# Two stores per block, behind the first or behind the second transposing transfer of a retention and MLP kernel

## The chip, the cores and the metric

The kernel runs on one core of a Trainium2 chip. The metric is the device time of one launch in microseconds (us). Before the change the median of three runs is 190.57 us (190.29 to 191.04).

## The reference

Per batch and head a state of 64 x 64 is decayed and fed with an outer product of k and v, position by position; q reads it. The heads are then put side by side, and an MLP with the activation h * tanh(softplus(h)) follows.

```python
batch, n_heads, seq, head_dim = (4, 8, 768, 64)
...
for t in range(S):
    state = gamma * state + einsum('bhd,bhe->bhde', k[:, :, t], v[:, :, t])
    y[:, :, t] = scale * einsum('bhd,bhde->bhe', q[:, :, t], state)
...
x = y.transpose(0, 2, 1, 3).reshape(B * S, H * D)     # 3072 x 512
h = x @ w_in                                          # 512 -> 2048
sp = where(h > 20.0, h, log1p(exp(minimum(h, 20.0))))
out = (h * tanh(sp)) @ w_out                          # 2048 -> 512
```

Inputs and output are fp32; the products inside are made from fp16 operands.

## The kernel before, in words

**Chunks and blocks.** The 768 positions of a batch are 6 chunks of 128 positions with all 8 heads, so there are 24 chunks (`NCK`), numbered g. A block is the unit of the MLP: block 0 has four chunks, blocks 1 to 10 have two each, and `first[b]` is a block's first chunk (`first[4]` = 10, `first[5]` = 12, and so on). `ONE` = 3, `BACK` = 4 and `DEFER` = 6 are numbers of blocks at which the order changes.

**A chunk's way in.** SP (SyncE) issues a chunk's loads of q, k and v from HBM (`load_one`, L174; tiles `qf`, `kf`, `vf`, four buffers each). GpSimd casts them to fp16 with their scales (`casts_qk`: q on L440, k on L454; `casts_v`: L459). Then SP issues one transposing DMA from the cast q and k to the tile `qkt` (`turn_by_dma`, L464), which gives q and k with head dimensions on the partitions. It waits for the cast of k. The scores (`score`, L507, tile `at`) and the products with the state (`past_of`, `y_mm` L621) read `qkt`; the outer products (`u_ps`, L515) read the cast k and v.

**A block from number 4 on.** The main loop calls `second_of(blk - 1)`, then `full_in`, then `full_out`. `full_in` makes the hidden layer (`h_ps`, L972, seven products in place of eight by sums of quarters, 112 matmuls) with its activation on ScalarE. `full_out` makes the output (`o_ps`, L1214, seven products of eight matmuls each), and in the midst of it the retention work of coming blocks: `retain(blk + 1, blk + 2)` makes y of the next block and the outer products and scores of the block after that. Sums that need two products run on VectorE, the evacuations on ScalarE and VectorE. TensorE's order is the order in which the program is written.

**The output.** `full_out` takes two tiles `osb` of 128 x 512 fp32 (256 KB, nine buffers), fills them, and appends them to the list `stores`. Nothing is sent to HBM at that place: `store(n)` takes the n oldest of the list and has SP issue them (L1498), and `store_due` takes all that are due (L244). From block 4 on, the two that are taken are those of two blocks before.

**SP's queue.** SP issues in program order, loads, transposing transfers and stores alike; an issue that waits holds what is behind it. Two functions set the order here, with g = `first[blk]` + 6:

- `next_one(g)`, called in the midst of `full_out(blk)`: the transfer of chunk g; in block 6 also the loads of v of two chunks; then two stores (blocks 4 to 7), or all that are due (from block 8 on).
- `second_of(blk)`, called between `full_out(blk)` and `full_in(blk + 1)`: a load, GpSimd's casts of q and k of chunk g + 1, its transfer, GpSimd's casts of v, then two stores in block 3 alone, or all that are due (from block 8 on), and another load.

So blocks 4, 5, 6 and 7 carry the transfers of chunks 16 and 17, 18 and 19, 20 and 21, 22 and 23. The loads of a whole chunk are five DMAs as a rule, and eight for chunks 19 and 21, whose k comes in four parts and whose q comes in two. In block 5, the two loads of `second_of` bring q and k of chunks 20 and 21 alone.

Of the kernel before, what the change touches and what calls it, by code (L numbers as in the profile page):

```python
# [16 lines left out]
def kernel(  # L17
# [15 lines left out]
    NCK = B * NCH  # L33
# [4 lines left out]
    first = [sum(BLOCKS[:i]) for i in range(len(BLOCKS))]  # L38
# [84 lines left out]
    ONE, BACK = 3, 4  # L123
# [40 lines left out]
    def load_one(g, n, queue):  # L164
        b, c = divmod(g, NCH)
        small = g in (first[8] + 1, first[9] + 1)
        if n == 0:
            src, parts = pair_src(q, *divmod(g, 2)), 2 if small else 1
        else:
            src = (k, v)[n - 1][b, :, c * C:(c + 1) * C].rearrange("h p d -> p h d")  # L170
            parts = 1 if g < first[6] else 4 if small and n == 1 else 2
        size = src.shape[1] // parts
        for h in range(0, src.shape[1], size):
            queue.dma_start(loaded[g][n][:, h:h + size], src[:, h:h + size])  # L174

    def load(g):
        room(g)
        for n in range(3):
            load_one(g, n, nc.sync)

    def load_to(g):
        while nload[0] < min(g, NCK):
            load(nload[0])
            nload[0] += 1
# [56 lines left out]
    def store_due(now):  # L241
        while stores and stores[0][0] <= now:
            _, dst, osb = stores.pop(0)
            nc.sync.dma_start(dst, osb)  # L244
# [189 lines left out]
    def casts_qk(g, now=True):  # L434
        qf = loaded[g][0]
        qk16 = castp.tile([P, 2, H, D], FP16, name="qk16", bufs=4)
        q16, k16 = qk16[:, 0], qk16[:, 1]
        v16 = castp.tile([P, H, D], FP16, name="v16", bufs=7)
        heads = slice(g % 2 * (H // 2), (g % 2 + 1) * (H // 2))
        nc.gpsimd.tensor_tensor(  # L440
            in_place(q16.rearrange("p (w x) d -> p w x d", x=2)), by_head(qf),
            scale_by_head(qs_two[:, heads]), op=ALU.mult)
        cast[g] = (q16, k16, v16, qk16)
        if now:
            cast_k(g)
# [12 lines left out]
    def casts_v(g):  # L458
        nc.gpsimd.tensor_tensor(  # L459
            cast[g][2], loaded.pop(g)[2], vs[g % 2].unsqueeze(2).broadcast_to((P, H, D)), op=ALU.mult)  # L460

    def turn_by_dma(g):
        qkt = qktp.tile([P, H, C], FP16, name="qkt", bufs=6)
        nc.sync.dma_start_transpose(qkt, cast[g][3].rearrange("p a h d -> p (a h d)"))  # L464
        qkts[g] = (qkt[:, :HP].rearrange("p (i r) c -> p i r c", r=2), qkt[:, HP:])
# [727 lines left out]
    def full_out(blk, last):  # L1193
# [56 lines left out]
        if last:  # L1250
            mm(px, s(2), t(2))
            u2 = snap(px)
            pb = bank()
            mm(pb, a(0, 1), b(1, 0), True)
            sums_c(blk)
            done(0, 0, pb, m1)
        else:
            leave(new)
            if later is None:
                mm(px, s(2), t(2))  # L1260
                u2 = snap(px)
                retain(new)
            pb = bank()
            mm(pb, a(0, 1), b(1, 0), True, halved=halved[2])
            if later is None:
                sums_c(blk)
                done(0, 0, pb, m1)
                finish(new, False)
            else:
                done(0, 0, pb, m1)  # L1270
                sums_c(blk)
                cast_behind(blk, 3)
                mm(px, s(2), t(2))
                u2 = snap(px)
                retain(new, later)
                mask_two(later)
            next_one(first[blk] + 6)
# [217 lines left out]
    def store(n):  # L1495
        for _ in range(n):
            _, dst, osb = stores.pop(0)
            nc.sync.dma_start(dst, osb)  # L1498
# [8 lines left out]
    def next_one(g):  # L1507
        if g < first[ONE] + 8:
            load_to(g + 3)
        if g < NCK:  # L1510
            turn_by_dma(g)
        if g == first[DEFER] + 6:
            for n in range(2):
                load_one(g + n, 2, nc.sync)
            nload[0] = g + 2
        if g >= NCK:
            store_due(NFB)
        elif g >= first[ONE] + 8:
            store(2)

    def load_qk(g):
        room(g)
# [3 lines left out]
    def second_of(blk):  # L1526
        g = first[blk] + 6
        load, ahead = (load_qk, -1) if blk + 1 == DEFER else (load_to, 0)
        if blk != DEFER:
            load(g + 3 + ahead)  # L1530
        if g < NCK:
            nc.gpsimd.tensor_copy(summed, xts[blk + 1][:, 3, TB - 1:])
            casts_qk(g + 1)
            turn_by_dma(g + 1)
            casts_v(g)
            casts_v(g + 1)
        if blk == ONE:
            store(2)
        elif g >= NCK:
            store_due(NFB)  # L1540
        load(g + 4 + ahead)

# [64 lines left out]
    for blk in range(1, len(BLOCKS)):  # L1607
        last = blk + 1 == len(BLOCKS)
        if blk >= BACK:
            second_of(blk - 1)  # L1610
            full_in(blk, last)
            full_out(blk, last)
            continue
# [5 lines left out]
        for u in range(0 if blk in FULL else NFB // 2):  # L1619
# [7 lines left out]
            for _ in range(SUMS_AT[blk].count(u)):  # L1627
                input_sums.pop(0)()
        later = blk + 2 if blk == ONE else None
        hooks = [([(leave, blk + 1)] if later is not None else []) + [(retain, blk + 1, later)],  # L1630
                 [(next_one, first[blk] + 6)] if blk + 1 >= BACK else
                 [(turn_load, first[blk] + 4)] if blk == 1 else
                 [(turn_four, first[blk] + 4)],
# [35 lines left out]
```

## Time and profile before

| | before |
|---|---|
| median of three runs | 190.57 us (190.29 to 191.04) |
| the profiled execution | 190.19 us, of which the span of instructions 188.4 us |
| TensorE clock granted | 1.00 |
| matmuls / weight loads busy | 182.7 us / 162.9 us |
| VectorE / ScalarE / GpSimd busy | 148.2 / 113.0 / 66.8 us |
| SP's DMA queue | 38.22 MB, 84.9% of the 16 DMA engines' span |

A row of the profile names the line of the kernel, the engine, the operation and the tiles (written <- read). PE is TensorE's matmuls, PEld its weight loads, SPq the queue of SyncE, whose time is the time to issue and not to move the data. All times in the profile count from the first instruction. "DMA to landing" is from the start of the issue to the last byte's signal.

### The profile page before, as it was taken

The page shows a single profiled execution, that of the slowest core. Times are in us where ns is not written, and L with a number is a line of the kernel's source. Part 1 is how long each engine was busy: PE and PEld are TensorE (multiplying, and loading weights), DVE is VectorE, ACT ScalarE, POOL GpSimd, SP SyncE. Part 2 cuts the span into 40 slices and gives each one's busy share as a digit, 9 for nine tenths or more (in the row PEclk, how much of TensorE's full clock was granted, in tenths as well). Part 3 has the DMA queues.
Part 4 walks back from the last instruction along what each step waited for, and adds up shares of the span by engine and source line. Part 5 has one row for each costly group of instructions (what it writes and reads, how often), then busy time and mean ns, then how long its engine had stood idle before and what let it go on. Part 6 is the DMA issues. An engine that isn't in the chain of part 4 may idle for free.

```text
span 188.4 us, 7968 instructions
## 1 busy us (share of the span) xinstructions
PE 182.7 (97%) x3438; PEld 162.9 (86%) x3438; DVE 148.2 (79%) x318; ACT 113.0 (60%) x217; POOL 66.8 (35%) x95
## 2 busy tenths in 40 slices
PE   7998999999999999999999999999999999999993
PEld 7756478888998998998998998998998998988983
DVE  0888599998987998997897697687698698666862
ACT  3575776264555583884684583683673773874651
POOL 5072000588607516532354714714624800000000
PEclk9999999999999999999999999999999999999999
DMA  5999999999899999999799997993999990301103
GB/s 169 306 313 387 387 385 368 298 322 212 171 249 213 188 250 141 175 244 206 197 159 270 192 195 150 181 262 67 218 221 228 203 336 34 117 3 48 67 3 111
DMA packets 83236, 38.84 MB, mean 206 GB/s; under 512 B 58241, under 2 KB 76289, under 8 KB 83201
## 3 DMA queue, kind: packets, MB, share of 16 engines
q1 hardware_dynamic: 82912, 38.22, 84.9%
q8 instruction: 27, 0.44, 1.0%
q10 hardware_dynamic: 288, 0.11, 0.2%
q14 instruction: 9, 0.07, 0.1%
HBM read 27.31 MB, written 6.29 MB: 178 GB/s over the span
## 4 chain that ended last, share of the span: by engine, by line
PE 92%; DMA 3%; SPq 1%; POOL 1%; issue 1%; ACT 0%; DVE 0%; POOLq 0%; DVEq 0%
PE h_ps L972 30%; PE o_ps L1214 23%; PE o_ps L1097 10%; PE h_ps L753 8%; PE o_ps L810 7%; PE y_ps L621 3%; DMA kf<-in_k_dram 3%; PE h_ps L700 2%; PE u_ps L515 1%; PE at L507 1%; PE y_ps L399 1%; POOL qk L320 1%; PE h_ps L736 1%; PE t_ps L267 1%; PE at L350 1%
## 5 line engine op out<-in xcount | busy, mean ns | idle before, releaser
L972 PE MATMUL h_ps<-xt,wsum 128*128 128x128 f16 x576 | 37.5, 219 | 0.0
L984 ACT ACTIVATE g<-h_ps 128x512 f16<-128x512 f32 x54 | 30.8, 599 | 7.1 <-PE h_ps L972 7.1
L972 PEld LDWEIGHTS <-wsum 128*128 128x128 f16 x576 | 33.6, 98 | 0.0
L972 PE MATMUL h_ps<-xt,win 128*128 128x128 f16 x432 | 31.2, 219 | 0.0
L972 PEld LDWEIGHTS <-win 128*128 128x128 f16 x432 | 26.4, 98 | 0.4
L1214 PEld LDWEIGHTS <-gsum 128*128 128x128 f16 x232 | 21.5, 98 | 2.6
L1214 PE MATMUL o_ps<-tmat,gsum 128*128 128x256 f16 (+1 forms) x176 | 21.5, 268 | 0.0
L1045 DVE TENSOR_TENSOR h_ps<-h_ps,hsum 128x512 f32<-128x512 f32 x18 | 12.5, 692 | 9.4 <-PE h_ps L972 9.3
L459 POOL TENSOR_TENSOR v<-vf,qvs 128x512 f16<-128x512 f32 x18 | 19.2, 1082 | 1.1 <-DMA vf<-in_v_dram 1.0
L440 POOL TENSOR_TENSOR qk<-qf,qvs 128x512 f16<-128x512 f32 x18 | 18.9, 1053 | 0.7 <-DMA qf<-in_q_dram 0.7
L1015 ACT COPY h_ps<-h_ps 128x512 f32<-128x512 f32 x18 | 10.5, 582 | 13.4 <-issue 8.6
L1214 PEld LDWEIGHTS <-g 128*128 128x128 f16 x184 | 16.5, 97 | 1.6
L679 ACT CAST xt<-y_ps 128x512 f16<-128x512 f32 x16 | 10.8, 738 | 9.4 <-PE y_ps L621 9.4
L753 PE MATMUL h_ps<-xt,win 128*128 128x256 f16 (+2 forms) x164 | 16.3, 260 | 0.0
L753 PEld LDWEIGHTS <-win 128*128 128x128 f16 x164 | 13.4, 98 | 2.7
L1568 POOL COPY summed<-gsum 128x1 f16<-128x1 f16 x7 | 1.6, 235 | 39.4 <-DVE gsum L933 32.2
L1224 ACT COPY snap<-o_ps 128x256 f32<-128x256 f32 (+1 forms) x22 | 8.2, 374 | 11.0 <-PE o_ps L1214 11.0
L762 ACT ACTIVATE g<-h_ps 128x512 f16<-128x512 f32 x18 | 10.7, 597 | 6.5 <-PE h_ps L753 6.5
L1214 PE MATMUL o_ps<-wout,g 128*128 128x256 f16 (+1 forms) x120 | 14.5, 265 | 0.0
L997 DVE TENSOR_TENSOR hsum<-h_ps,hsum 128x512 f32<-128x512 f32 x18 | 12.3, 685 | 0.9 <-PE h_ps L972 0.2
L454 POOL TENSOR_TENSOR qk<-kf,qvs 128x512 f16<-128x512 f32 x12 | 12.8, 1070 | 0.3 <-DMA kf<-in_k_dram 0.3
L810 PEld LDWEIGHTS <-g 128*128 128x128 f16 x120 | 11.4, 98 | 1.6
(130 smaller groups left out, 348.6 us busy)
## 6 DMA issues: line engine op xcount, KB each, us to landing
out_dram<-osb SPq DMA_DIRECT2D x22, 256.0 KB, 3.7
qf<-in_q_dram SPq DMA_DIRECT2D x18, 256.0 KB, 5.4
kf<-in_k_dram SPq DMA_DIRECT2D x14, 256.0 KB, 5.8
vf<-in_v_dram SPq DMA_DIRECT2D x14, 256.0 KB, 5.3
wt<-in_moe_w_out_dram SPq DMA_DIRECT2D x6, 512.0 KB, 8.6
vf<-in_v_dram SPq DMA_DIRECT2D x20, 128.0 KB, 4.1
wi<-in_moe_w_in_dram SPq DMA_DIRECT2D x4, 512.0 KB, 8.8
kf<-in_k_dram SPq DMA_DIRECT2D x16, 128.0 KB, 4.3
```

What stands on the lines that cost most here:

```text
L440: nc.gpsimd.tensor_tensor(in_place(q16.rearrange("p (w x) d -> p w x d", x=2)), by_head(qf), scale_by_head(qs_two[:, heads]), op=ALU.mult)
L454: nc.gpsimd.tensor_tensor(dst, src, boosts.rearrange("p (w y) -> p w y", y=2).unsqueeze(3).broadcast_to((P, H // 2, 2, D)), op=ALU.mult)
L459: nc.gpsimd.tensor_tensor(cast[g][2], loaded.pop(g)[2], vs[g % 2].unsqueeze(2).broadcast_to((P, H, D)), op=ALU.mult)
L679: nc.scalar.copy(dst[:, :, x], src)
L753: nc.tensor.matmul(h_ps[:, j, cols], wins[s][f // 2][:, bp, f % 2 * P:(f % 2 + 1) * P], xts[blk][:, bp, cols], start=(bp == 0 and at == 0) ...
L810: nc.tensor.matmul(banks[ij][:, t], x(f)[:, t * P:(t + 1) * P], w(f), start=ij in open_banks, stop=f == fs[-1], skip_group_check=True)
L972: nc.tensor.matmul(o_ps[:, f], w(f // 2, k)[:, f % 2 * P:(f % 2 + 1) * P], x[:, k], start=begin and f == 0 and k == 0, stop=k == 1, skip_g ...
L984: nc.scalar.activation(gt[:, f:f + n, j * C:(j + 1) * C], src, AF.Mish, scale=inv_boost3)
L997: nc.vector.tensor_tensor(m, src, plus, op=ALU.add)
L1045: nc.vector.tensor_tensor(pf[p], pa[p], m5[p], op=ALU.add)
L1097: nc.tensor.matmul(o_ps[:, cols], x(f), w(f)[:, cols], start=first and z == 0, stop=z == n - 1, skip_group_check=True)
L1214: nc.tensor.matmul(o_ps[:, c:c + wide], x(f), w(f)[:, c:c + wide], start=first and f == 0 and c == cols.start, stop=f == n - 1, skip_group ...
```

## The change

In blocks 4 to 7 the call `store(2)` leaves `next_one`, where it stood behind the transfer of chunk g, and stands in `second_of`, behind the transfer of chunk g + 1. In block 3 it stood there already. Blocks 8 and later keep `store_due` in both functions. The number of instructions, of DMAs and of bytes stays as it is.

```diff
     def next_one(g):
...
         if g >= NCK:
             store_due(NFB)
-        elif g >= first[ONE] + 8:
-            store(2)
...
     def second_of(blk):
...
             turn_by_dma(g + 1)
             casts_v(g)
             casts_v(g + 1)
-        if blk == ONE:
+        if g < NCK:
             store(2)
-        elif g >= NCK:
+        else:
             store_due(NFB)
         load(g + 4 + ahead)
```

## The prediction

> **What bounds the kernel now.** I began with the page: its engine shares, the chain of work that ended last, and the groups.
>
> ```profile
> span 188.4 us, 7968 instructions
> ...
> PE 182.7 (97%) x3438; PEld 162.9 (86%) x3438; DVE 148.2 (79%) x318; ACT 113.0 (60%) x217; POOL 66.8 (35%) x95
> ...
> PE 92%; DMA 3%; SPq 1%; POOL 1%; issue 1%; ACT 0%; DVE 0%; POOLq 0%; DVEq 0%
> ...
> L1214 PEld LDWEIGHTS <-gsum 128*128 128x128 f16 x232 | 21.5, 98 | 2.6
> ...
> out_dram<-osb SPq DMA_DIRECT2D x22, 256.0 KB, 3.7
> ```
>
> TensorE is busy for 97% of the span and holds 92% of the chain. SP's queue, the one that the change reorders, holds 1% of the chain, and a DMA 3%. So a reordered queue can change the end only where it makes TensorE wait, or ends a wait that TensorE has now. The last two rows are used below: one weight load of the output matmuls takes 98 ns, and one store is 256 KB, so the moved pair is 512 KB.
>
> Next I read the busy time by stretches, for the output halves (`full_out`) of blocks 4 and 7. Each row gives the stretch, its length, then each engine's busy time, the granted clock, the DMA share and GB/s.
>
> ```profile
> 97.00:104.60 7.60, 7.60 (x180) 6.69 (x179) 6.42 (x17) 3.69 (x8) 2.19 (x3) 1.00 0.92 226
> ...
> 138.60:146.00 7.40, 7.40 (x180) 6.53 (x179) 6.48 (x17) 3.63 (x8) 2.19 (x3) 1.00 1.06 228
> ```
>
> TensorE is busy for the whole of both stretches, at clock 1.00. The weight loads fill less, 6.69 of 7.60 us and 6.53 of 7.40 us; what that is worth is weighed under the change. The DMA engines are full too (shares of 0.92 and 1.06 at 226 to 228 GB/s), so a store of 512 KB is not free in DMA time: 0.524 MB at 226 GB/s is 2.3 us of it.
>
> Then the chain in order of time, to see when TensorE reads what the transposing transfers write. Those readers are the `at` matmuls (L507): in block b they score the chunks of block b + 2.
>
> ```profile
> 110.94 3.51 PE o_ps L1214 x32
> 114.45 0.51 PE y_ps L621 x48
> 114.95 0.26 PE u_ps L515 x21
> ...
> 115.25 0.27 PE at L507 x26
> ...
> 115.68 2.73 PE o_ps L1214 x24
> 118.41 6.30 PE h_ps L972 x112
> ...
> 129.08 0.32 PE at L507 x32
> ...
> 142.80 0.29 PE at L507 x32
> ...
> 156.45 0.03 PE at L507
> ```
>
> The pieces follow one another without a hole. Chunks 16 and 17 are read from about 115.2 us, 18 and 19 from 129.1, 20 and 21 from 142.8, 22 and 23 from 156.45.
>
> **The change, part by part.** It adds and removes no instruction. In each of blocks 4 to 7, SP's queue holds: transfer of chunk g, two stores, loads, transfer of chunk g + 1, loads. After the change the two stores stand behind the second transfer. Here is SP's queue before, in order (start, time to issue, line, how many merged).
>
> ```profile
> 105.28 1.00 SPq L1498 DMA_DIRECT2D out_dram<-osb  x2
> 106.33 0.44 SPq L174 DMA_DIRECT2D qf<-in_q_dram  x1
> ...
> 111.05 1.51 SPq L464 DMA_TRANSPOSE qkt<-qk  x1
> 112.61 1.11 SPq L174 DMA_DIRECT2D qf<-in_q_dram  x2
> ...
> 118.91 2.00 SPq L1498 DMA_DIRECT2D out_dram<-osb  x2
> ...
> 122.67 1.75 SPq L464 DMA_TRANSPOSE qkt<-qk  x1
> ...
> 134.48 0.93 SPq L1498 DMA_DIRECT2D out_dram<-osb  x2
> 135.52 1.44 SPq L464 DMA_TRANSPOSE qkt<-qk  x1
> 137.01 1.27 SPq L174 DMA_DIRECT2D qf<-in_q_dram  x1
> ...
> 146.62 1.00 SPq L1498 DMA_DIRECT2D out_dram<-osb  x2
> 148.53 1.47 SPq L464 DMA_TRANSPOSE qkt<-qk  x1
> 150.09 1.01 SPq L244 DMA_DIRECT2D out_dram<-osb  x2
> ```
>
> A transfer cannot be issued before GpSimd has cast its chunk's k, so the second thing to read is when the casts of the odd chunks end:
>
> ```profile
> 106.18 1.04 POOL L454 TENSOR_TENSOR qk<-kf,qvs 128x512 f16<-128x512 f32 x1
> ...
> 120.01 1.04 POOL L454 TENSOR_TENSOR qk<-kf,qvs 128x512 f16<-128x512 f32 x1
> ...
> 133.84 1.04 POOL L454 TENSOR_TENSOR qk<-kf,qvs 128x512 f16<-128x512 f32 x1
> ...
> 147.46 1.05 POOL L454 TENSOR_TENSOR qk<-kf,qvs 128x512 f16<-128x512 f32 x1
> ```
>
> They end at 107.22, 121.05, 134.88 and 148.51 us.
>
> *What moves earlier.* Chunk 17: SP is free of the pair's 1.05 us (105.28 to 106.33), so its transfer goes from 111.05 to 110.0, and no further forward than 107.2 if the 2.3 us of DMA data ahead of it also shortens the issue of the loads between. Chunk 19: the pair held SP for 2.0 us, but the cast ends at 121.05, so 1.6 us earlier. Chunk 21: 135.52 to 134.88, 0.6 us earlier. Chunk 23: it starts 0.02 us after its cast, so nothing. The loads between the two transfers of blocks 4 and 5 move up with them.
>
> *What moves later.* The pair itself, by 1.5 to 6 us; nobody on the chip reads the stored rows again. Its tiles come from nine buffers, of which each block takes two, and before block 5's output half asks for its two, both orders have issued the same stores; the stored tiles are those of two blocks earlier, long written. So no tile wait is added. The loads behind the second transfer: chunk 19's begin at 110.0 + 1.56 + 1.05 = 112.61, as now. Chunk 21's begin at 121.05 + 1.8 + 2.0 = 124.9, which is 0.4 us later than behind a transfer at 122.67 that takes 1.75. Chunks 22 and 23 begin at 134.88 + 1.49 + 1.04 = 137.4 in place of 137.01: 0.4 us later. The remaining stores start near 151.1 in place of 150.09, 37 us before the end. The bounds for the delay of a load behind the pair are 0 (the same bytes stand ahead of it in both orders) and 2.3 us (the pair's whole DMA time); I take 0.4, from SP's rows, because no load passes a store that it did not pass before.
>
> *What the earlier transfers are worth.* When each landed is in the answers on the transfers' line; the first two lines below are of chunk 17's issue alone, the third is over all 18 transfers.
>
> ```profile
> L464 SPq DMA_TRANSPOSE qkt<-qk x1: 1512/1512/1512, 111.0 to 111.0; - x1
> DMA to landing us min/median/max: 3.7/3.7/3.7
> ...
> DMA to landing us min/median/max: 3.1/4.0/5.9
> ```
>
> Chunk 17 lands at 111.05 + 3.7 = 114.75 and is read from 115.25: 0.5 us in hand, the tightest of the four. With the slowest landing of all, 5.9 us, chunk 19 lands at 128.6 for 129.1, chunk 21 at 141.4 for 142.8, chunk 23 at 154.4 for 156.45. No transfer is late today, so landing one earlier is worth 0. Bounds: below, what TensorE could still have hidden there. In block 5 `u` and `at` take 115.52 less 114.95, under 0.6 us, for 64 matmuls; a hidden wait there cannot exceed that, and the 0.32 us of block 6 for 32 `at` alone says that it is close to none.
>
> *What the later loads cost.* The tightest is chunk 23's k, the last of its two halves:
>
> ```profile
> L174 SPq DMA_DIRECT2D kf<-in_k_dram x1: 714/714/714, 142.1 to 142.1; - x1
> DMA to landing us min/median/max: 4.6/4.6/4.6
> ```
>
> It lands at 146.7 and GpSimd needs it at 147.46: 0.76 us in hand against 0.4. Past that the transfer of chunk 23 would be late, and it has 156.45 less (148.53 + 5.9), at least 2.0 us, in hand (with the median of 4.0, 3.9 us). So the loads cost 0; even the bound of 2.3 us makes the transfer 1.5 us late, which the 2.0 us covers.
>
> *The weight loads.* The rows leave TensorE's weight loads idle for 0.91 us of block 4's output half and 0.87 of block 7's. Of this, 56 output matmuls at 3.51/32 = 0.110 us (block 5's piece) against a load of 0.098 us explain 56 x 0.012 = 0.65 us: a load waits under each wide matmul, whatever SP does. The Trainium skill (Perfetto Trace Analysis, Identifying the Most-Contended Engine) calls matmul busy time a bad measure of headroom and has the busy share of the weight loads read instead. By that rule the four output halves could still hold up to about 3.6 us of headroom, where the busy rows say none; this trace puts most of it under the matmuls' own pace.
>
> **Sum.** 0 on TensorE from the earlier transfers, 0 from the later loads, 0 from the later stores: the profiled execution stays at its own 190.19 us (span 188.4 and 1.8 around it). The median of the runs is 190.57, 0.38 above, so I predict 190.6 us.
>
> **The rivals.**
>
> *A wait inside the busy time goes (faster).* For it: chunk 17 has only 0.5 us in hand, and the weight loads are idle for 0.9 us in each output half. Of four halves with 0.9 us, 0.65 each belongs to the pace; the 0.25 left gives 4 x 0.25 = 1.0 us, so 189.6. Against it: only chunks 17, 19 and 21 move at all, chunk 19 and 21 had time in hand, and the same idle 0.87 us stands in block 7, where nothing tight is read. The page's rule taken whole would give 190.6 - 3.6 = 187.0. Chance 0.08.
>
> *The loads behind the pair come too late (slower).* The place is chunk 23's k and its transfer. The price is one us of TensorE for each us that the transfer lands after 156.45. It begins to cost at a delay of 0.76 + 2.0 = 2.8 us, and passes 0.5% (about 0.95 us, which is about what a measurement of this kernel can tell from no change) at 3.7 us: 191.5 and above; at 5 us, 192.8. For it: the DMA engines are full in these stretches, so an order that costs DMA time shows at once, and GpSimd's casts, in order, pass a delay on to the casts of v behind them. Against it: 0.4 us worked out, 2.3 at the bound. Chance 0.12.
>
> *The transfer does not move.* Where GpSimd's cast gates it, as for chunk 23, the change only puts the stores 1 us later. If that holds for all four: 190.6 again, inside the forecast.
>
> **How the numbers follow.** No change 0.80 (the third rival in it), faster 0.08, slower 0.12; these are also the chances of over 0.5% either way. The forecast's own range is the spread of the runs around it, 190.3 to 191.0. The range goes from 189.7, almost all that the idle 0.25 us in four blocks gives, to 191.5, where the late loads begin to count as slower; what lies beyond is left to the two rivals, at most 0.2 together.
>
> **What would show it.** Right: in the profile after, the transfers of chunks 17, 19 and 21 start about 1.0, 1.6 and 0.6 us earlier, chunk 23's stays at its cast, the `h_ps` pieces still take 6.30 us for 112, and TensorE is busy for all of each stretch. Wrong towards faster: the stretch of `y_ps`, `u_ps` and `at` in block 5 is shorter than 1.2 us (114.45 to 115.68), or the 3.51 us pieces shrink. Wrong towards slower: GpSimd waits for a kf or qf in block 7, chunk 23's transfer lands past 156.45, and a gap opens before `at` in block 8. My reading fails if the span moves by more than 0.9 us while TensorE's pieces keep their lengths.

## The result and the profile after

The changed kernel takes 190.94 us in the median of 20 runs, the kernel before 190.32 us in 20 runs beside it. The ratio of the runs is 1.0026, 95% interval [1.0014, 1.0038] (these two medians alone would give 1.0033): about 0.5 us slower (0.0026 x 190.32), within the 0.5% that was called no change, and not nothing.

The page of the changed kernel, the rows that answer to the first ones of before:

```profile
span 189.2 us, 7968 instructions
...
PE 183.3 (97%) x3438; PEld 162.6 (86%) x3438; DVE 149.9 (79%) x318; ACT 113.1 (60%) x217; POOL 66.6 (35%) x95
...
PE 92%; DMA 3%; DVE 2%; ACT 1%; issue 1%; SPq 0%; DVEq 0%
```

TensorE still holds 92% of the chain, but VectorE, which had a rounded 0% of it, now holds 2%. The chain in order of time says where. First the kernel before, block 7, from the start of its hidden layer to that of the next:

```profile
132.29 6.30 PE h_ps L972 x112
138.59 3.51 PE o_ps L1214 x32
142.10 0.44 PE y_ps L621 x40
...
145.95 6.30 PE h_ps L972 x112
```

Then the changed kernel, the same stretch:

```profile
132.55 4.93 PE h_ps L972 x88
...
137.50 0.69 DVE hsum L997
138.19 0.33 DVE mid L567
138.52 0.97 DVE gsum L924
...
139.51 0.42 DVE gsum L925
139.93 0.35 DVE gsum L924
...
140.33 2.36 PE o_ps L1214 x20
142.68 0.44 PE y_ps L621 x40
...
146.54 6.30 PE h_ps L972 x112
```

The chain leaves TensorE at 137.5, runs through five VectorE operations, and comes back at 140.33. The stretch takes 146.54 - 132.55 = 13.99 us in place of 145.95 - 132.29 = 13.66: 0.33 us lost in one place. The view of the waits names it (us in total, number of waits, longest). The kernel before has neither of the first two rows in this stretch, and 1.0 us in the last:

```profile
PEld L1214 <- DVE gsum L924: 0.4, 1, 0.4
PE o_ps L1214 <- DVE gsum L924: 0.2, 1, 0.2
...
POOL v L459 <- DMA vf<-in_v_dram: 2.0, 2, 1.3
```

TensorE waits for VectorE's first sum of block 7 (`sums_a`, L924), and GpSimd waits longer for v. The timeline of the two engines, kernel before first (a bracket gives how long the engine sat idle before, and what ended that):

```profile
135.85 2.11 POOL L459 TENSOR_TENSOR v<-vf,qvs 128x512 f16<-128x512 f32 x2 [0.97 <-DMA vf<-in_v_dram]
138.18 0.41 DVE L924 TENSOR_TENSOR gsum<-g 128x512 f16<-128x512 f16 x1
```

and the changed kernel:

```profile
135.79 1.04 POOL L459 TENSOR_TENSOR v<-vf,qvs 128x512 f16<-128x512 f32 x1 [0.67 <-DMA vf<-in_v_dram]
138.15 1.04 POOL L459 TENSOR_TENSOR v<-vf,qvs 128x512 f16<-128x512 f32 x1 [1.32 <-DMA vf<-in_v_dram]
138.44 1.04 DVE L924 TENSOR_TENSOR gsum<-g 128x512 f16<-128x512 f16 x1
```

Before, GpSimd's second cast of v ended at 137.96, and VectorE's sum began 0.2 us later and took 0.41 us. After, the cast runs from 138.15 to 139.19; the sum begins inside it and takes 1.04 us. The two share no data: the one reads v of chunk 21, the other the activations of block 7.

Why the cast is late is in SP's queue and in the landing of the last of the four v loads. Kernel before (the queue of that place stands in the prediction; the loads of v are issued from 132.12), then the changed one:

```profile
L174 SPq DMA_DIRECT2D vf<-in_v_dram x1: 510/510/510, 133.9 to 133.9; - x1
...
DMA to landing us min/median/max: 2.9/2.9/2.9
```

```profile
132.43 2.26 SPq L174 DMA_DIRECT2D vf<-in_v_dram  x4
135.15 1.23 SPq L464 DMA_TRANSPOSE qkt<-qk  x1
136.48 1.44 SPq L1498 DMA_DIRECT2D out_dram<-osb  x2
137.97 0.44 SPq L174 DMA_DIRECT2D qf<-in_q_dram  x1
...
L174 SPq DMA_DIRECT2D vf<-in_v_dram x1: 505/505/505, 134.2 to 134.2; - x1
DMA to landing us min/median/max: 3.8/3.8/3.8
```

In block 6 alone, loads of v stand right behind the first transfer (`DEFER`). Before, two stores followed them; now the transfer of chunk 21 does. The last load is issued 0.3 us later (134.2 for 133.9) and lands at 138.0 in place of 136.8. The whole stretch starts 0.26 us later in this profile (132.55 for 132.29), VectorE's sum with it; so what brings the two together is the other 0.9 us, the longer time to landing.

The profiled spans differ by 0.8 us, more than the runs do. Part of the rest is not shown to belong to any store: a start of block 6's hidden layer that waits for nothing shown is in the changed kernel (first row) and, longer, in the first experiment below (second row), which up to that point issues everything as the kernel before does.

```profile
118.47 0.39 PEld L972 LDWEIGHTS <-win 128*128 128x128 f16 x7 [0.20 <-issue]
...
118.50 0.45 PEld L972 LDWEIGHTS <-win 128*128 128x128 f16 x8 [0.37 <-issue]
```

### The profile page after: what moved, and what is told of

Its sections match the earlier page's. It is cut to its first block, busy times and chain, and to the rows that moved or that the text cites. A ratio compares the mean times of both kernels' runs of the same rounds, so it can differ in the third digit from the quotient of the medians.

```text
span 189.2 us, 7968 instructions
## 1 busy us (share of the span) xinstructions
PE 183.3 (97%) x3438; PEld 162.6 (86%) x3438; DVE 149.9 (79%) x318; ACT 113.1 (60%) x217; POOL 66.6 (35%) x95
## 4 chain that ended last, share of the span: by engine, by line
PE 92%; DMA 3%; DVE 2%; ACT 1%; issue 1%; SPq 0%; DVEq 0%
PE h_ps L972 29%; PE o_ps L1214 23%; PE o_ps L1097 10%; PE h_ps L753 8%; PE o_ps L810 7%; PE y_ps L621 3%; DMA qfirst<-in_q_dram 3%; PE h_ps L700 2%; PE at L507 1%; PE t_ps L267 1%; PE u_ps L515 1%; PE at L350 1%; PE y_ps L399 1%; PE h_ps L736 1%; DVE gsum L924 1%; PE at L478 1%
## 5 line engine op out<-in xcount | busy, mean ns | idle before, releaser
L1237 DVE TENSOR_TENSOR osb<-o_ps,snap 128x256 f32<-128x256 f32 (+1 forms) x22 | 9.1, 414 | 4.5 <-ACT snap L1224 2.8
```

## The experiments

The theory from here on (A): the loss is made in block 6 and paid in block 7. The transfer, moved up behind the loads of v, delays the last of them; GpSimd's cast of it meets VectorE's sum; the sum waits; TensorE waits for the sum. Against it stood B, a loss spread over the four blocks, and C, no effect of the order at all.

All ten, each timed against the kernel before on the same chip. "Block 7" is the stretch from the start of block 7's hidden layer to that of block 8, in the profiled execution; "longest sum" is the longest of that block's four 128 x 512 sums (L924, L925).

| kernel | ratio, 95% interval | block 7, us | longest sum, us |
|---|---|---|---|
| before | | 13.66 | 0.42 |
| the change | 1.0026 [1.0014, 1.0038] | 13.99 | 1.04 |
| e1, block 6 alone | 1.0022 [1.0010, 1.0035] | 14.10 | 1.15 |
| e2, all but block 6 | 1.0015 [0.9999, 1.0032] | 13.66 | 0.42 |
| e3, the change, v first | 1.0010 [0.9995, 1.0026] | 13.67 | 0.42 |
| e4, before, v later | 1.0022 [1.0013, 1.0032] | 13.97 | 1.15 |
| e5, before, v first | 1.0000 [0.9988, 1.0011] | 13.67 | 0.42 |
| e6, block 6 alone, v first | 0.9995 [0.9984, 1.0006] | 13.67 | 0.43 |
| e7, blocks 4 and 5 alone | 1.0008 [0.9995, 1.0020] | 13.67 | 0.42 |
| e8, block 7 alone | 1.0005 [0.9989, 1.0020] | 13.67 | 0.42 |
| e9, an extra cast on GpSimd | 1.0009 [0.9994, 1.0024] | 13.92 | 0.96 |
| e10, extra writes on GpSimd | 0.9995 [0.9981, 1.0009] | 13.67 | 0.42 |

The column of the stretch has two values: 13.66 to 13.67 in the eight kernels without a long sum, 13.92 to 14.10 in the four with one.

**Block 6 alone, and all but block 6.** e1, against the kernel before:

```diff
-        elif g >= first[ONE] + 8:
+        elif g >= first[ONE] + 8 and g != first[DEFER] + 6:
             store(2)
...
-        if blk == ONE:
+        if blk in (ONE, DEFER):
             store(2)
```

> The kernel before, with the two stores moved behind the second transfer in block 6 alone. Theory A (one place: in block 6 the transfer of chunk 21 now stands right behind the loads of v, the last v lands about 1.2 us later, GpSimd's cast of v of chunk 21 runs at about 138.2 in place of 136.9 us and holds up VectorE's first gsum sum of block 7, which took 1.04 us in place of 0.41, and TensorE waits about 0.3 us): the whole loss is here, ratio 1.0015 to 1.0035, that gsum sum over 0.8 us, the last GpSimd cast of v before it starting after 137.5. Theory B (the loss is spread over the four blocks, about 0.1 us each): ratio about 1.0006. Theory C (the difference is in how two programs happen to run, not in the order of the stores): ratio 1.000.

e2, against the kernel before:

```diff
-        elif g >= first[ONE] + 8:
+        elif g == first[DEFER] + 6:
             store(2)
...
-        if blk == ONE:
+        if g < NCK and blk != DEFER:
             store(2)
```

> The change without block 6: in blocks 4, 5 and 7 the stores stand behind the second transfer, in block 6 behind the first as before. Theory A: ratio 1.000 within 0.001, all gsum sums of 128x512 near 0.42 us. Theory B: three quarters of the loss, 1.002. Theory C: 1.0026 as for the whole change, or 1.000.

e1 is as slow as the whole change within the noise, 1.0022 [1.0010, 1.0035], and its timeline shows the same meeting, one sum later:

```profile
138.44 0.41 DVE L924 TENSOR_TENSOR gsum<-g 128x512 f16<-128x512 f16 x1
138.53 1.23 POOL L459 TENSOR_TENSOR v<-vf,qvs 128x512 f16<-128x512 f32 x1 [1.44 <-PE h_ps L972]
138.89 1.15 DVE L925 TENSOR_TENSOR gsum<-gsum,g 128x512 f16<-128x512 f16 x1
```

The bracket names a matmul, but the last load of v landed at 138.37 (issued at 134.13, 4.24 us to landing), and the cast starts 0.16 us after that, as it does in the changed kernel (137.99 and 138.15). So block 6 alone brings a loss that cannot be told from the whole. e2 has no long sum and no longer block 7, but its ratio, 1.0015 [0.9999, 1.0032], reaches both theories' values: inconclusive on the time.

**The parts of the others.** e7 keeps the moved stores in blocks 4 and 5 (`elif g >= first[DEFER] + 6` in `next_one`, `if ONE <= blk < DEFER` in `second_of`), e8 in block 7 (`elif first[ONE] + 8 <= g <= first[DEFER] + 6`, `if blk in (ONE, DEFER + 1)`).

> The stores moved in blocks 4 and 5 alone. Theory A: 1.000 within 0.0012. Theory B: 1.0012 or more.

> The stores moved in block 7 alone. Theory A: 1.000 within 0.0012; the transfer of chunk 23 still starts at its cast. Theory B: 1.0006 or more, if the last stores, one us later, hold something up.

1.0008 [0.9995, 1.0020] and 1.0005 [0.9989, 1.0020]: neither is told from 1, and B's 1.0012 for e7 is inside its interval. What blocks 4, 5 and 7 cost stays open up to 0.2%, the upper end of both intervals.

**The same loss with no store moved behind a transfer.** e4, against the kernel before; block 6's later `store(2)` is left out:

```diff
         if g == first[DEFER] + 6:
+            store(2)
             for n in range(2):
                 load_one(g + n, 2, nc.sync)
```

> The kernel before, with block 6's two stores issued one step earlier, between the transfer of chunk 20 and the loads of v, so that v lands later while no store is moved behind any transfer. Theory A: v of chunk 21 lands one to two us later, its cast meets VectorE's gsum sums of block 7, and the kernel is slower by 0.2 to 0.4 us: ratio 1.001 to 1.003. Theories B and C: nothing is moved behind a transfer, so 1.000 or a little under.

It is slower by 1.0022 [1.0013, 1.0032]. The second cast of v starts at 139.14, and the last of the four sums is long:

```profile
139.14 1.16 POOL L459 TENSOR_TENSOR v<-vf,qvs 128x512 f16<-128x512 f32 x1 [1.28 <-DMA vf<-in_v_dram]
139.44 1.15 DVE L925 TENSOR_TENSOR gsum<-gsum,g 128x512 f16<-128x512 f16 x1
```

What counts is not where the stores stand but when v lands.

**The loss taken away.** In block 6 SP waits for a cast before the first transfer, and the loads of v need nothing then. e3 (against the changed kernel), e5 (against before) and e6 (against e1) issue them there:

```diff
-        if g < NCK:
-            turn_by_dma(g)
         if g == first[DEFER] + 6:
             for n in range(2):
                 load_one(g + n, 2, nc.sync)
             nload[0] = g + 2
+        if g < NCK:
+            turn_by_dma(g)
```

> The changed kernel, with block 6's loads of v of chunks 20 and 21 issued ahead of the transfer of chunk 20 in place of behind it, where SP waits for a cast. Theory A: v lands before 134 us, GpSimd casts v right behind k (from about 135.1 to 137.2 us), the meeting with VectorE's gsum sums is gone, and so is the loss: ratio 0.999 to 1.0005. Theory B: the loss stays at three quarters or more, 1.002 to 1.0026. Theory C: any.

> The kernel before, with block 6's loads of v issued ahead of the transfer of chunk 20. Theory A: v casts run right behind k (about 135 to 137 us), the 0.2 us by which they now miss VectorE's gsum sum becomes about 1 us; 0.998 to 1.0005, a gain only if some executions of the kernel before do collide. Theory B (the stores' places in all blocks): 1.000.

> Block 6's stores moved behind the second transfer, and its loads of v ahead of the first; the other blocks as before. Theory A: the loss of the move in block 6 (1.0022) is gone: 0.999 to 1.0008, all gsum sums near 0.42 us. If the move in block 6 cost by another way, such as later loads of chunks 22 and 23: 1.0015 to 1.0025.

e6 against e1 is the clearest pair: the same stores behind the same transfer, 0.9995 [0.9984, 1.0006] in place of 1.0022 [1.0010, 1.0035]. In e6 both casts of v run right behind k's, and the sum that begins at 138.10 meets nothing:

```profile
134.74 2.04 POOL L459 TENSOR_TENSOR v<-vf,qvs 128x512 f16<-128x512 f32 x2
138.10 0.41 DVE L924 TENSOR_TENSOR gsum<-g 128x512 f16<-128x512 f16 x1
```

Its loads of chunks 22 and 23 start at 137.99, as late as in the changed kernel (137.97), so those loads are cleared of the loss. Theory C falls too: the loss came with the meeting in e1 and e4, and went with it in e6. e3 is at 1.0010 [0.9995, 1.0026], between the theories on the time, with block 7 back at 13.67. e5 changes nothing, 1.0000 [0.9988, 1.0011]: the kernel before misses the meeting by 0.2 us in its profile, which is enough. No version beat the kernel before by more than the noise.

**GpSimd's part by itself.** e9 and e10 leave every DMA of the kernel before in its place. After block 6's casts of v, e9 repeats the last one into the same tile, and e10 writes an old table three times:

```diff
             casts_v(g)
+            vf = loaded[g + 1][2]
             casts_v(g + 1)
+            if blk == DEFER:
+                nc.gpsimd.tensor_tensor(
+                    cast[g + 1][2], vf, vs[(g + 1) % 2].unsqueeze(2).broadcast_to((P, H, D)),
+                    op=ALU.mult)
```

```diff
             casts_v(g)
             casts_v(g + 1)
+            for _ in range(3 if blk == DEFER else 0):
+                nc.gpsimd.memset(keep_four, 0.0)
```

> The kernel before, stores and DMAs untouched; in block 6 GpSimd repeats its cast of v of chunk 21, which reads SBUF for about 1.04 us more, from about 138.0 to 139.0 us. If a GpSimd operation that reads SBUF holds up VectorE's gsum sum (two operands in SBUF), that sum takes over 0.9 us in place of 0.41, ends 0.2 to 0.4 us after GpSimd's operation, and the kernel is slower by 0.2 to 0.4 us: ratio 1.001 to 1.0025. If the loss comes from the DMA traffic around the moved stores and GpSimd has no part in it: 1.000, all gsum sums near 0.42 us.

> The kernel before, stores and DMAs untouched; in the same place of block 6 GpSimd writes a table that is no longer used three times (memset, about 0.31 us each), reading nothing. If VectorE's sum is held up by GpSimd's reads alone: all gsum sums near 0.42 us, ratio 1.000 within 0.001. If any GpSimd operation holds it up: a gsum sum of 0.5 to 0.8 us, ratio up to 1.002.

e9's timeline, then e10's:

```profile
137.84 1.04 POOL L1539 TENSOR_TENSOR v<-vf,qvs 128x512 f16<-128x512 f32 x1
138.20 0.96 DVE L924 TENSOR_TENSOR gsum<-g 128x512 f16<-128x512 f16 x1
```

```profile
138.07 1.06 POOL L1538 MEMSET keep_four<- 128x256 f32 x3
138.47 0.42 DVE L924 TENSOR_TENSOR gsum<-g 128x512 f16<-128x512 f16 x1
```

An operation that reads SBUF holds the sum up, 0.96 us in place of 0.41, and block 7 takes 13.92 us; writes over the same stretch of time do not touch it. The profile decides here: e9's ratio, 1.0009 [0.9994, 1.0024], holds both the expected loss and none. In all four meetings VectorE's sum ends 0.28 to 0.29 us after GpSimd's operation by the rows above (139.48 for 139.19 in the changed kernel, 140.04 for 139.76 in e1, 140.59 for 140.30 in e4, 139.16 for 138.88 in e9). It began 0.29 to 0.36 us behind GpSimd's start in each. For another distance there are two earlier meetings, in the kernel before as in all the others. One of them, with TensorE's row of the chain around it:

```profile
77.52 1.04 POOL L440 TENSOR_TENSOR qk<-qf,qvs 128x512 f16<-128x512 f32 x1
77.55 1.29 DVE L580 TENSOR_TENSOR sth<-suh,gch 128x256 f16<-128x256 f32 x1
...
76.19 5.41 PE h_ps L972 x96
```

This product of two SBUF tiles takes 0.425 us in the median of the kernel before. Here it begins 0.03 us behind GpSimd's start, takes 1.29 us, and again ends 0.28 us after GpSimd's end (78.84 for 78.56). (The other, from 63.73, takes 0.95 us.) So it is a wait for the whole operation and then most of the sum's own 0.41 us, not two operations that share a rate. The chain stays on TensorE throughout, so TensorE does not wait for this one; in block 7 it waits for the sum. GpSimd is held up in the same way when it comes second: in e1 and e4 its cast began inside a sum (138.53 in the sum from 138.44 to 138.85; 139.14 in the one from 138.99 to 139.41) and took 1.23 and 1.16 us in place of 1.04.

The Trainium skill (SBUF — State Buffer, Who interferes with whom) states this: a VectorE instruction with two SBUF inputs contends with a GpSimd instruction that reads SBUF, not with one that only writes it, and the contention is an exclusive lock in which the order of issue decides who blocks. e9 and e10 agree, 0.96 us against 0.42.

## Why the prediction was right, and where it was not

**The time and the class.** 190.6 us was forecast, in 189.7 to 191.5 us, with "no change" at 0.80; 190.94 came out. Of the sum's three zeros the one for the later loads should have been 0.33 us by the profile: the term that was mis-sized is *what moves later*, read too narrowly. That the path which it left out cost less than 0.5% is luck, since nothing in the sum priced it.

**The step that failed.** That part followed the loads behind the second transfer and stopped there, because "no load passes a store that it did not pass before". It did not ask what the moved-up transfer does to the loads ahead of it. In block 6 these are the loads of v; the queue quoted in the prediction jumps from the transfer of chunk 19 to the stores at 134.48 and leaves them out. And GpSimd's cast was priced only by who reads v later, never by who runs beside it: the 0.2 us between its end and VectorE's sum was not looked at. The busy times by stretch could not show it, since a held-up sum counts as busy. None of the signs named for a slower outcome came, as all of them watched chunk 23; what failed among the signs of being right was that TensorE is busy for all of each stretch (7.54 of 7.69 us in block 7's output half).

**The earlier transfers.** They are worth 0, as forecast. Where each starts, in the changed kernel, with the casts that gate chunks 19 and 23:

```profile
110.11 1.25 SPq L464 DMA_TRANSPOSE qkt<-qk  x1
...
119.97 2.05 SPq L174 DMA_DIRECT2D kf<-in_k_dram  x2
122.12 1.24 SPq L464 DMA_TRANSPOSE qkt<-qk  x1
123.46 1.05 SPq L1498 DMA_DIRECT2D out_dram<-osb  x2
124.56 1.10 SPq L174 DMA_DIRECT2D qf<-in_q_dram  x1
...
120.16 1.04 POOL L454 TENSOR_TENSOR qk<-kf,qvs 128x512 f16<-128x512 f32 x1
...
148.05 1.04 POOL L454 TENSOR_TENSOR qk<-kf,qvs 128x512 f16<-128x512 f32 x1
...
149.12 2.03 SPq L464 DMA_TRANSPOSE qkt<-qk  x1
```

Chunk 17 starts at 110.11 (110.0 was forecast), chunk 21 at 135.15 (134.88), chunk 23 at 149.12, 0.03 us after its cast, as before. Chunk 19 was off: 122.12, only 0.55 us earlier in place of 1.6, although its cast ended at 121.20. SP did not come free, since the loads of k between took until 122.02 (119.97 and 2.05), 2.05 us to issue in place of the 1.12 before (121.44 to 122.56).

**The later loads.** Chunk 21's start at 124.56 (124.9 was forecast); chunks 22 and 23's at 137.97 (137.4), 1.0 us later than before in place of 0.4. They cost nothing, as forecast; e6 shows it.

**The rivals.** *The loads come too late* had the sign and half of the mechanism: it said that GpSimd passes a delay on to its casts of v. It put the place at chunk 23 and the price behind 2.8 us of slack. The real place had 0.2 us of it, on an engine that was asked for no data. *A wait inside the busy time* found nothing: in kernels without the meeting block 7 stays at 13.66 to 13.67 us wherever the stores stand. *The transfer does not move* held for chunk 23 alone.

**Open.** e2, e3, e7 and e8 all lie a little above 1 (1.0015, 1.0010, 1.0008, 1.0005), and each has 1 inside its interval. Their mean is 1.0010, that of e5, e6 and e10 0.9997. Block 7's 0.33 us is 0.17% of the time, where the change cost 0.26%. So a further loss of some 0.1% outside this meeting is likelier than none, but no run shows it by itself, and its place is not known.

## What to carry to other kernels

When a DMA moves ahead of others in a queue, follow the transfers that it now crowds on both sides, to the engine operation that waits for their data, and then to what runs beside that operation. On this kernel GpSimd's casts and VectorE's sums of two SBUF operands hold each other up when they overlap. Where TensorE waits for the sum next, their distance in time is slack that belongs in the prediction's sum, 0.2 us here, like that of any semaphore. If it is short, issue the load where the queue stands idle anyway: e6 did so, and the place of block 6's stores no longer mattered.

## What the runs showed of the hardware that was not expected

- A GpSimd operation that reads SBUF stops a VectorE sum of two SBUF operands until it is done: 0.41 us became 0.96 to 1.15 us in four profiles; three writes of 0.31 to 0.32 us each did nothing to it (0.42 us).
- The last load ahead of a transposing transfer took longer to land. Where a transfer is the next DMA behind block 6's loads of v, the last of them took 3.8 to 4.2 us (the change, e1, e3, e4, e6); where stores come next, 2.7 to 2.9 us (before, e2, e7, e9, e10). The profiles of e5 and e8 lack this landing. In the kernel before, the second store stands in that place: 4.0 us against 2.9 for the first, and nothing waits for it. How these share the DMA engines no run here shows.
